# Attention, gated product and routed experts in one kernel: a unit's scores ahead of older transposes, masks on VectorE, another plan for conversions

## The chip, the cores and the metric

One core of one Trainium2 chip. The metric is device time in microseconds (us), the median of three runs. Engines are named as in the profile: PE is TensorE's matmul stream (PEld its weight loads), DVE is VectorE, ACT is ScalarE, POOL is GpSimd, SP is SyncE, which issues transfers.

## The reference

Three stages run one after the other; each consumes what the one before produced.

```
mask = q_bucket[:, :, :, None] == k_bucket[:, :, None, :]
scores = np.where(mask, scale * (q @ k^T), -1e9)          # 2 x 8 heads, 768 x 768, depth 64
attn = exp(scores - max); attn = attn / (sum + 1e-09); out = attn @ v
...
x = (a * b) @ w_out,  a = x @ w_a,  b = x @ w_b          # 1536 tokens, 512 -> 1536 -> 512, 64-bit weights
...
logits = normalised x @ normalised expert_emb / tau; one expert of 8 for each token
out[mask] = gate * (relu(x[mask] @ w1[e]) @ w2[e])       # 512 -> 1024 -> 512
```

A bucket is the signs of six projections. A query without a key in its bucket has all scores at -1e9, and so takes the mean of all v.

## The kernel before, in words

Attention is cut into 48 units: a pair of heads (8 pairs), one of the two heads, 256 of the 768 queries; six units belong to a pair, and r is the unit's number within it. A unit u has two halves t of 128 queries. The main loop makes one step for each u, and in it works on several units at once:

- `scores(u, t)` (lines 244 and 245, tile `st`): four matmuls, two chunks of keys, each with a second matmul that adds the mask through feature rows;
- `rowmax` (L254, DVE), `expo` (L260, ACT): row maximum, exponential and row sum `su`;
- `masked` (L267, L269): from the row maximum, `mk` (1 where the query has a key in its bucket) and `mc` (1/S where it hasn't); `recip` (L276, DVE): 1/sum; `normal` (L280, L282, POOL): s = r * mk, then e = e * s + mc on 128x768, twice;
- `etrans(u, m)`, m = 0, 1, 2 (L290): four transposes of e into a PSUM tile; `ehigh` (L300, ACT) and `elow` (L304, DVE) split it into a high and a low part for the product with v, `pv` (L316);
- `epilogue` and `finish` (L331, L332 on ACT; L340, xh, L342 on POOL): the two partial products of an older unit are added and split into x's high and low parts;
- in the same loop, work for the next pair: its q and k are transposed (`pt`, L162), split (L167, L170) and turned into bucket bits (`z`, L213; `ft`, L219), and v is split (`splv`, POOL); `hook(u, k)` runs steps of other jobs at five places of a step.

The jobs on hooks are four conversions of 64-bit weights to pairs of fp32r parts for the gated product, seven steps each: rest, top, low, size, guard on DVE (L542 to L561), add (L553) on POOL, and parts (L567) on ACT and POOL. A planner in `jobs` put them over steps u = 5 to 46, the POOL steps where r is 0 or 4.

Step u issues, in PE's order: scores(u, 0), the second transposes of unit u-2, scores(u, 1), the first product of unit u-3, the third transposes of u-2, the rest of u-3's product, the next pair's `pt` or `z`, and last the first transposes of unit u-1, which read what POOL's L282 writes in the same step.

Ahead of the loop the opening loads k and q of the first pair, stacks high and low parts (L372, L373), transposes them (L381), projects them (L392) and writes feature rows (L395); 28 transposes of the identity run first (`warm`, L364). After attention the gated products run (L636, L648 to L662), then the router (L767 to L854; `pos` is the place of a token in its expert's list, `sel` and `slots` the lists), the gathers (L890), their transposes (`xgt`, L906), and the experts (`hp` L929, `op` L979, result `o` L986, scattered by L987).

Every engine works in the order in which the program issues. There is no run-time scheduler.

Of the kernel before, what the change touches and what calls it, by code (L numbers as in the profile page):

```python
# [8 lines left out]
F32 = mybir.dt.float32  # L9
# [12 lines left out]
def f32(ap):  # L22
    return ap.bitcast(F32)


class Kernel:
# [69 lines left out]
    def features0(self):  # L96
        nc = self.nc
        NF, NB, D = self.NF, self.NF // 2, self.D
        pr, pp = self.pr, self.pp
        nc.vector.tensor_copy(pp[:, 0], pr)  # L100
        nc.vector.tensor_tensor(pp[:, 1], pr, f32(pp[:, 0]), ALU.subtract)
        for t in range(2):

            d = slice(D * t, D * t + D)
            for n, sign in enumerate((1.0, -1.0) if t == 0 else (-1.0, 1.0)):
                o = slice(D + n * NB, D + (n + 1) * NB)
                nc.gpsimd.tensor_scalar(self.lz0[:, t, 0, o], f32(pp[:, 0]), sign, None, ALU.mult)
                nc.gpsimd.tensor_scalar(self.lz0[d, t, 1, o], f32(pp[d, 1]), sign, None, ALU.mult)


    def attention(self, xh, xl, pools, hook):
# [121 lines left out]
        def small(tag):  # L233
            return sb.tile([128, 2], F32, tag=tag, name=tag, bufs=4)
# [29 lines left out]

        def masked(u):
            f = small("mk")
            nc.gpsimd.tensor_scalar(f, NM[u], BIG / 2, 1.0, ALU.is_lt, ALU.mult)  # L267
            c = small("mc")
            nc.gpsimd.tensor_scalar(c, NM[u], BIG / 2, 1.0 / S, ALU.is_ge, ALU.mult)  # L269
            MK[u] = (f, c)  # L270

        R = {}

        def recip(u):
            R[u] = small("r")
            nc.vector.reciprocal(R[u], SU.pop(u))  # L276

        def normal(u):
            r, (f, c) = small("s2"), MK.pop(u)
            nc.gpsimd.tensor_tensor(r, R.pop(u), f, ALU.mult)  # L280
            for t in range(2):
                nc.gpsimd.tensor_scalar(E[u, t], E[u, t], r[:, t:t + 1], c[:, t:t + 1], ALU.mult, ALU.add)  # L282

        def etrans(u, m):
            pt = ps_t.tile([128, 512], F32, tag="t", name="et")
            for cc in range(2):
                for t in range(2):
                    e = E[u, t].rearrange("p a b -> p (a b)")
                    c = 2 * m + cc
                    nc.tensor.transpose(  # L290
                        pt[:, (2 * cc + t) * 128:(2 * cc + t + 1) * 128],
                        e[:, c * 128:(c + 1) * 128], self.ident,
                    )
            eh = sb.tile([128, 512], F32R, tag="eh", name="eh", bufs=5)
            el = sb.tile([128, 512], F32R, tag="el", name="el", bufs=5)
            ET[u, m] = (eh, el, pt)
# [56 lines left out]
                return f(i + 1, *args)  # L353
            return None

        load(0, "k")
        load(0, "q", nc.scalar)
        for d in (0, 64):
            nc.gpsimd.dma_start(out=self.pr[d:d + 64], in_=self.proj)
        hook(-1, 0)  # L360

        warm = ps_t.tile([128, 512], F32, tag="t", name="warm")
        for m in range(28):
            nc.tensor.transpose(warm[:, m % 4 * 128:m % 4 * 128 + 128], self.ident, self.ident)  # L364

        P[0, 0] = sb.tile([128, 4, S], F32R, tag="p", name="p", bufs=2)
        p = P[0, 0]
        stacks = []
        for nm, h, scale in (("k", 1, 1.0), ("q", 0, float(D) ** -0.5)):
            s = sb.tile([128, NC, 2, D], F32R, tag="splv", name="stack", bufs=3)  # L370
            r = raw[0, nm][:, :, 0, :]
            nc.scalar.mul(s[:, :, h, :], r, scale)  # L372
            nc.vector.scalar_tensor_tensor(s[:, :, 1 - h, :], r, scale, f32(s[:, :, h, :]), ALU.mult, ALU.subtract)  # L373
            stacks.append(s)
        self.features0()
        for t, s in zip((1, 0), stacks):
            for half in range(2):
                pt = ps_t.tile([128, 512], F32, tag="t", name="pt0")
                for m in range(3):
                    c = 3 * half + m  # L380
                    nc.tensor.transpose(  # L381
                        pt[:, m * 128:(m + 1) * 128], f32(s[:, c]).rearrange("p a d -> p (a d)"), self.ident
                    )
                cols = slice(384 * half, 384 * half + 384)
                nc.scalar.copy(p[:, t, cols], pt[:, :384])
                nc.vector.tensor_copy(p[0:D, 2 + t, cols], pt[D * t:D * t + D, :384])
        for t in (1, 0):
            z = ps_s.tile([128, 2, 512], F32, tag="s", name="z0")
            for half in range(2):
                cols = slice(384 * half, 384 * half + 384)  # L390
                for m in range(2):
                    nc.tensor.matmul(  # L392
                        z[:D + NF, half, :384], self.lz0[:, t, m], p[:, t, cols], start=(m == 0), stop=(m == 1)
                    )
            nc.vector.tensor_scalar(  # L395
                p[D:D + NF, 2 + t].rearrange("p (a b) -> p a b", a=2), z[D:D + NF, :, :384],
                self.thr0[D:D + NF, t:t + 1], 1.0 if t == 0 else -BIG, ALU.is_gt, ALU.mult,
            )
        self.features()
        load(1, "qk")  # L400

        opening = [[(nm, half) for half in range(2)] for nm in "qk"]
        for u in range(NU + 4):
# [2 lines left out]
            act, last, tr, out = u < NU, 0 <= u - 1 < NU, 0 <= w < NU, 0 <= x < NU  # L406
            if act:
                scores(u, 0)
            if y >= 0:
                epilogue(y)  # L410
            prep = chunk(u) if 0 < u < NU else None
# [24 lines left out]
            if act:  # L436
                rowmax(u, 1)
                masked(u)
            if u == 0:
                for args in opening[1]:  # L440
                    for g in prep_t(0, *args):
                        g()
                stack_parts(0, 1, "k")
                load(0, "v")
                load(1, "v")
                hook(-1, 1)
# [32 lines left out]
                load(i + 2)  # L479
            elif r >= 4 and i + 1 < len(pairs):  # L480
                stack(i + 1, r - 4)
            if last:
                etrans(u - 1, 0)
            if act:
                expo(u, 1)
            if tr:
# [19 lines left out]
class Experts:  # L506
# [16 lines left out]
    def split64(self, src, shape, dest, scratch=None):  # L523
# [30 lines left out]


        def size():
            nc.vector.tensor_scalar(T["lo"], T["hi"], 0x7FFFFFFF, None, ALU.bitwise_and)

        def guard():
            v = f32(T["v"])  # L560
# [407 lines left out]
    def expert_out(self, e, b, n):  # L968
# [14 lines left out]
        if n < 3:  # L983
            return
        o = self.ex.tile([128, self.DM], F32, tag="o", name="o", bufs=2)
        nc.scalar.mul(o, p, self.sg[b][:, e:e + 1])  # L986
        nc.gpsimd.indirect_dma_start(  # L987
            out=self.K.out, out_offset=bass.IndirectOffsetOnAxis(ap=self.so[b][:, e:e + 1], axis=0),
            in_=o, in_offset=None, bounds_check=self.B * self.S - 1, oob_is_err=False,
# [108 lines left out]
def tile_kernel(ctx, tc, q, k, v, proj, w_a, w_b, w_out, emb, tau, w1, w2, out, dbg=None):  # L1098
# [5 lines left out]
    with tc.manual_schedule():  # L1104
# [15 lines left out]
        with tc.tile_pool(name="conv", bufs=1, side="left") as X.conv, \  # L1120
# [8 lines left out]
            def late():  # L1129
# [4 lines left out]


            plan = {(-1, 0): [jobs[0][0], jobs[1][0]], (NU - 5, 1): [j[0] for j in outs]}
            streams = [
                {"steps": [(step, m) for _, steps in jobs[n::2] for m, step in enumerate(steps)], "ready": 4,
                 "fetch": jobs[2 + n][0]} for n in range(2)
            ]  # L1140
            for u in range(4, NU):
                r = u % 6
                if r == 2:
                    continue
                for stream in streams:
                    steps = stream["steps"]
                    if steps and u >= stream["ready"] and (steps[0][1] in (3, 6)) == (r in (0, 4)):
                        step, m = steps.pop(0)
                        plan[u, 3 if m in (3, 6) else 4] = [step]
                        if m == 6 and steps:  # L1150
                            at = next(x for x in range(u + 2, u + 9) if x % 6 in (0, 1))
                            plan[at, 0] = [stream["fetch"]]
                            stream["ready"] = at + 3
                        break
                streams.reverse()
            assert not any(stream["steps"] for stream in streams)
            r, o = [j[1] for j in outs]

            def both(*steps):
                return lambda: [step() for step in steps]  # L1160

            tail = [
                r[0], r[1], both(*r[2:4]), o[0], o[1], both(*r[4:6]), both(*o[2:4]), r[6], both(*o[4:6]), o[6],
            ]
            first = [(t, f, w, h) for t in range(2) for f in range(2) for w in range(2) for h in range(2)]


# [37 lines left out]
        def after(name, fn, *args):  # L1205
            side.setdefault(name, []).append(lambda: fn(*args))
# [92 lines left out]
        def begin():  # L1299
# [4 lines left out]
        chain(("o", L, 0, 2), [(T, 0), (T, 1), [(R, 0), (T, 2)], (R, 1), (R, 2)], 2)  # L1304
        chain(("o", L, 1, 2), [
            (T, 3), (T, 4), [(R, 3), (T, 5), (X.route_norm, 0)], (R, 4), [(R, 5), (X.route_choose, 0)],
            None, None, (X.route_places, 0), None, None, [(X.route_slots, 0), (X.gather, 0, 0)],
            (X.route_gates, 0), None, None, None, None, None, (X.route_gate_slots, 0),
        ])
        chain(("o", L, 2, 1), [(T, 6), (T, 7), [(R, 6), (T, 8)], (R, 7), (R, 8)])  # L1310
# [6 lines left out]
        after(("t", 0, 0, 0), X.route_places, 1)  # L1317
        chain(("e", 0, 0, 0), [[(X.route_slots, 1), (X.gather, 0, 1)]])
        after(("h", 0, 1, 0), X.route_gates, 1)
        after(("e", 0, 0, 2), X.transpose_in, 0, 1)  # L1320
        after(("e", 0, 0, 3), X.gather, 1, 1)
        after(("e", 0, 1, 0), X.route_gate_slots, 1)
        after(("e", 0, 1, 0), X.transpose_in, 1, 0)
        after(("e", 0, 1, 1), X.transpose_in, 1, 1)
# [47 lines left out]
```

## Time and profile before

| | |
|---|---|
| median of 3 runs | 781.36 us (780.84 to 782.38) |
| the profiled execution | 781.89 us; its span 780.1 us, so 1.8 us lie outside the span |
| mean granted TensorE clock | 0.999 |
| PE busy | 756.1 us, 97% of the span |
| DVE, ACT, POOL busy | 63%, 53%, 62% |
| opening, attention | 0 to about 27 us, about 27 to 265 us |
| gated products, router, experts | to about 520, 610 and 773 us |

PE's busy time is modelled: the duration of a matmul reaches beyond the start of the next. What PE needs for a stretch is therefore read from the distance of starts in stretches without a wait, and not from the busy share. In the rows a time in brackets is the idle time of an engine just before an instruction and what ended it.

### The profile page before, as it was taken

The page shows a single profiled execution, that of the slowest core. Times are in us where ns is not written, and L with a number is a line of the kernel's source. Part 1 is how long each engine was busy: PE and PEld are TensorE (multiplying, and loading weights), DVE is VectorE, ACT ScalarE, POOL GpSimd, SP SyncE. Part 2 cuts the span into 40 slices and gives each one's busy share as a digit, 9 for nine tenths or more (in the row PEclk, how much of TensorE's full clock was granted, in tenths as well). Part 3 has the DMA queues.
Part 4 walks back from the last instruction along what each step waited for, and adds up shares of the span by engine and source line. Part 5 has one row for each costly group of instructions (what it writes and reads, how often), then busy time and mean ns, then how long its engine had stood idle before and what let it go on. Part 6 is the DMA issues. An engine that isn't in the chain of part 4 may idle for free.

```text
span 780.1 us, 13215 instructions
## 1 busy us (share of the span) xinstructions
PE 756.1 (97%) x4778; PEld 698.7 (90%) x4778; DVE 494.9 (63%) x793; ACT 414.4 (53%) x795; POOL 486.1 (62%) x532
## 2 busy tenths in 40 slices
PE   7999999999999999999999999999999999999996
PEld 6789988999889899999999999999998898899995
DVE  6789888898888754364654655533653755556551
ACT  4798898898888733321212222124343755564651
POOL 3788889889898957265463563644341865565651
PEclk9999999999999999999999999999999999999999
DMA  7875555854540303022111130053252666676620
GB/s 173 189 152 104 126 122 104 183 131 97 105 107 34 109 4 122 38 75 89 55 55 55 54 108 25 31 216 108 94 160 82 199 204 240 209 250 203 211 76 22
DMA packets 65347, 92.06 MB, mean 118 GB/s; under 512 B 28683, under 2 KB 32779, under 8 KB 65280
## 3 DMA queue, kind: packets, MB, share of 16 engines
q1 hardware_dynamic: 61088, 83.45, 38.8%
q0 software_dynamic: 2624, 7.35, 2.5%
q8 instruction: 39, 0.64, 0.3%
q10 hardware_dynamic: 1568, 0.39, 0.3%
q14 instruction: 28, 0.23, 0.1%
HBM read 66.08 MB, written 7.34 MB: 94 GB/s over the span
## 4 chain that ended last, share of the span: by engine, by line
PE 77%; POOL 11%; issue 5%; DVE 3%; ACT 1%; DMA 1%; POOLq 0%; SPq 0%; DVEq 0%; ACTq 0%
PE ab L636 24%; PE yp L662 12%; PE op L979 9%; PE hp L929 9%; POOL e L282 6%; PE et L290 6%; PE pv L316 4%; PE st L245 3%; PE st L244 3%; PE z L213 2%; PE hr L947 1%; PE lgp L745 1%; POOL xp L340 1%; PE xgt L906 1%; PE warm L364 1%
## 5 line engine op out<-in xcount | busy, mean ns | idle before, releaser
L636 PE MATMUL ab<-xh,w 128*128 128x384 f32 x768 | 204.1, 338 | 0.0
L636 PEld LDWEIGHTS ab<-xh,w 128*128 128x128 f32 x768 | 139.5, 188 | 0.8
L636 PE MATMUL ab<-xl,w 128*128 128x384 f32 x384 | 129.1, 336 | 0.0
L650 POOL TENSOR_TENSOR g<-a,g 128x384 fp32r<-128x384 f32 x48 | 52.6, 1096 | 105.2 <-ACT g L649 98.9
L885 POOL TENSOR_TENSOR w<-raw,w 128x1024 fp32r<-128x1024 f32 x36 | 87.5, 2432 | 35.2 <-ACT w L884 34.1
L254 DVE TENSOR_REDUCE nm<-st 128x1 f32<-128x768 f32 x96 | 91.3, 951 | 27.4 <-PE st L245 27.0
L290 PE MATMUL et<-ident,e 128*128 128x128 f32 x576 | 94.1, 277 | 9.9 <-POOL e L282 8.1
L662 PE MATMUL yp<-w,g 128*128 128x512 f32 x432 | 103.2, 391 | 0.3 <-POOL g L650 0.3
L304 DVE TENSOR_TENSOR el<-et,eh 128x512 fp32r<-128x512 f32 x144 | 95.3, 678 | 9.2 <-ACT eh L300 9.1
L282 POOL TENSOR_SCALAR e<-e,s,mc 128x768 f32<-128x768 f32 x96 | 94.5, 992 | 5.2
L300 ACT CAST eh<-et 128x512 fp32r<-128x512 f32 x144 | 84.5, 589 | 23.0 <-PE et L290 18.9
L662 PEld LDWEIGHTS yp<-w,g 128*128 128x128 f32 x432 | 80.4, 188 | 15.6 <-POOL g L650 0.8
L260 ACT ACTIVATE e<-st,nm 128x768 f32<-128x768 f32 x96 | 87.0, 906 | 5.0 <-DVE nm L254 2.0
L290 PEld LDWEIGHTS et<-ident,e 128*128 128x128 f32 x576 | 66.0, 140 | 22.6 <-POOL e L282 16.5
L649 ACT CAST g<-a 128x384 fp32r<-128x384 f32 x48 | 24.8, 516 | 110.4 <-DVE a L648 110.4
L979 PE MATMUL op<-w,hth 128*128 128x512 f32 x256 | 81.7, 400 | 0.0
L929 PE MATMUL hp<-xgh,w 128*128 128x256 f32 x448 | 80.7, 281 | 0.0
L316 PE MATMUL pv<-eh,splv 128*128 128x256 f32 x288 | 76.8, 296 | 0.0
L644 ACT COPY a<-ab 128x384 f32<-128x384 f32 x48 | 22.9, 478 | 97.2 <-PE ab L636 96.7
L244 PE MATMUL st<-p 128*128 128x384 f32 x192 | 73.0, 380 | 1.1 <-DVE p L395 0.7
L885 DVE TENSOR_TENSOR w<-raw,w 128x1024 fp32r<-128x1024 f32 x28 | 63.0, 2251 | 16.1 <-ACT w L884 16.1
L636 PEld LDWEIGHTS ab<-xl,w 128*128 128x128 f32 x384 | 72.3, 188 | 0.8
(192 smaller groups left out, 1549.9 us busy)
## 6 DMA issues: line engine op xcount, KB each, us to landing
raw<-in_moe_w_dram SPq DMA_DIRECT2D x32, 1024.0 KB
p<-hlq SPq DMA_DIRECT2D x15, 384.0 KB
p<-hlk SPq DMA_DIRECT2D x15, 384.0 KB
raw<-in_moe_w_a_dram SPq DMA_DIRECT2D x5, 1024.0 KB
raw<-in_moe_w_b_dram SPq DMA_DIRECT2D x5, 1024.0 KB
raw<-in_moe_w_out_dram SPq DMA_DIRECT2D x5, 1024.0 KB
raw<-in_k_dram SPq DMA_DIRECT2D x16, 192.0 KB
raw<-in_v_dram SPq DMA_DIRECT2D x16, 192.0 KB
```

Of the source, the lines that this page charges most:

```text
L244: nc.tensor.matmul(st[:, n, :384], p[:, 0, ql], p[:, 1, kl], start=True, stop=False)
L254: nc.vector.tensor_reduce(NM[u][:, t:t + 1], ST[u, t][:, :, :384], axis=AX.XY, op=ALU.max, negate=True)
L260: nc.scalar.activation(e, ST.pop((u, t))[:, :, :384], AF.Exp, bias=NM[u][:, t:t + 1], accum_out=SU[u][:, t:t + 1])
L282: nc.gpsimd.tensor_scalar(E[u, t], E[u, t], r[:, t:t + 1], c[:, t:t + 1], ALU.mult, ALU.add)
L290: nc.tensor.transpose(pt[:, (2 * cc + t) * 128:(2 * cc + t + 1) * 128], e[:, c * 128:(c + 1) * 128], self.ident,)
L304: nc.vector.tensor_tensor(el, pt, f32(eh), ALU.subtract)
L316: nc.tensor.matmul(p, w, parts[x][:, cc * 256:(cc + 1) * 256], start=(c == 0 and x == 0), stop=(c == NC - 1 and x == 1),)
L636: nc.tensor.matmul(p[:, :384], w[:, k, fs], x[:, k, cols], start=(k == 0 and n == 0), stop=(k == self.KD - 1 and n == 2),)
L662: nc.tensor.matmul(p, g[:, f, rows], w[:, f], start=(n == 0), stop=(n == 5))
L885: eng.tensor_tensor(l, raw, f32(h), ALU.subtract)
L929: nc.tensor.matmul(p[:, :256], w[:, k, fs], x[:, k], start=(n == 0), stop=(n == 3 * self.KD - 1))
L979: nc.tensor.matmul(p, h[:, 2 * n + f, rows], w[:, f], start=(n == 0 and f == 0 and m == 0), stop=(n == 3 and f == 1 and m == 2),)
```

## The change

- `etrans(w, 0)`, w = u-2, is issued just after `scores(u, 0)`. Before, the same transposes stood at the end of the step before, ahead of `scores(u, 0)`. Within `etrans` the half t is now the outer loop.
- `mk`, `mc` and the product s = r * mk are computed on DVE (L267, L269, L278 in the new numbering) and no longer on POOL.
- The planner of conversion steps is replaced by a table of steps u. POOL's steps stand at r = 0 only. For the jobs with a scratch buffer the step `size` is an Abs on ACT.
- Opening: k and q are loaded by head on two queues, with the projection between the halves (it was on POOL's queue); 22 warm transposes; queries of half 0 alone are stacked, turned and featured ahead of the first scores, and half 1 follows inside step 0.
- Router: places of tokens one slot later in the list that follows the last gated products; one transpose and one gather change places.
- The last result tile is scaled half on ACT and half on DVE.

```diff
         def masked(u):
-            nc.gpsimd.tensor_scalar(f, NM[u], BIG / 2, 1.0, ALU.is_lt, ALU.mult)
+            nc.vector.tensor_scalar(f, NM[u], BIG / 2, 1.0, ALU.is_lt, ALU.mult)
             c = small("mc")
-            nc.gpsimd.tensor_scalar(c, NM[u], BIG / 2, 1.0 / S, ALU.is_ge, ALU.mult)
+            nc.vector.tensor_scalar(c, NM[u], BIG / 2, 1.0 / S, ALU.is_ge, ALU.mult)
...
         def recip(u):
-            R[u] = small("r")
-            nc.vector.reciprocal(R[u], SU.pop(u))
+            r, (f, c) = small("r"), MK.pop(u)
+            nc.vector.reciprocal(r, SU.pop(u))
+            s = small("s2")
+            nc.vector.tensor_tensor(s, r, f, ALU.mult)
+            R[u] = (s, c)
...
-        for m in range(28):
+        for m in range(22):
...
+        stacked(1, slice(0, NC))
+        stacked(0, slice(0, 3))
+        self.features0()
+        for t, half in ((1, 0), (1, 1), (0, 0)):
+            turned(t, half)
+        featured(1, 0, 1)
+        featured(0, 0)
...
             if act:
                 scores(u, 0)
+            if tr:
+                etrans(w, 0)
...
             if u == 0:
+                stacked(0, slice(3, NC))
+                turned(0, 1)
+                featured(0, 1)
...
-            if last:
-                etrans(u - 1, 0)
...
         def size():
-            nc.vector.tensor_scalar(T["lo"], T["hi"], 0x7FFFFFFF, None, ALU.bitwise_and)
+            if scratch:
+                nc.scalar.activation(f32(T["lo"]), f32(T["hi"]), AF.Abs)
...
+            places = (
+                (3, 4, 5, 6, 6, 9, 12), (7, 10, 11, 12, 12, 13, 18), (17, 19, 21, 24, 24, 25, 36), (23, 27, 29, 30, 30, 31, 42),
+            )
...
-            None, None, (X.route_places, 0), None, None, [(X.route_slots, 0), (X.gather, 0, 0)],
+            None, None, None, (X.route_places, 0), None, [(X.route_slots, 0), (X.gather, 0, 0)],
...
-        after(("e", 0, 0, 2), X.transpose_in, 0, 1)
-        after(("e", 0, 0, 3), X.gather, 1, 1)
+        after(("e", 0, 0, 3), X.transpose_in, 0, 1)
+        after(("e", 0, 0, 2), X.gather, 1, 1)
```

On PE, from the last products of one step of the middle of attention to the second transposes of the next, before:

```order
261 L316 MATMUL pv<-el,splv 128x256
262 L290 MATMUL et<-ident,e 128x128 x4
263 L244 MATMUL st<-p 128x384
264 L245 MATMUL st<-p 128x384
265 L244 MATMUL st<-p 128x384
266 L245 MATMUL st<-p 128x384
267 L162 MATMUL pt<-ident,raw 128x128 x3
268 L290 MATMUL et<-ident,e 128x128 x4
```

And in the changed kernel:

```order
263 L318 MATMUL pv<-el,splv 128x256
264 L244 MATMUL st<-p 128x384
265 L245 MATMUL st<-p 128x384
266 L244 MATMUL st<-p 128x384
267 L245 MATMUL st<-p 128x384
268 L292 MATMUL et<-ident,e 128x128 x4
269 L162 MATMUL pt<-ident,raw 128x128 x3
270 L292 MATMUL et<-ident,e 128x128 x4
```

The four `st` matmuls of the next unit no longer stand behind the first four transposes of the unit before it.

On DVE one step from the reciprocal to the next row maximum, before (`spare` is a conversion step, not in every step):

```order
82 L276 RECIPROCAL r<-su 128x2
83 L304 TENSOR_TENSOR el<-et,eh 128x512 x2
84 L254 TENSOR_REDUCE nm<-st 128x1
85 L170 SCALAR_TENSOR_TENSOR hlk<-pt,hlk 128x384
86 L304 TENSOR_TENSOR el<-et,eh 128x512
87 L254 TENSOR_REDUCE nm<-st 128x1
```

And in the changed kernel:

```order
110 L276 RECIPROCAL r<-su 128x2
111 L278 TENSOR_TENSOR s_901<-r,mk 128x2
112 L306 TENSOR_TENSOR el<-et,eh 128x512 x2
113 L254 TENSOR_REDUCE nm<-st 128x1
114 L267 TENSOR_SCALAR mk<-nm 128x2
115 L269 TENSOR_SCALAR mc<-nm 128x2
116 L170 SCALAR_TENSOR_TENSOR hlk<-pt,hlk 128x384
117 L306 TENSOR_TENSOR el<-et,eh 128x512
118 L254 TENSOR_REDUCE nm<-st 128x1
```

Three small operations have come in, one ahead of the two `el` and two behind the second row maximum.

On POOL one step with `finish`, before:

```order
71 L267 TENSOR_SCALAR mk<-nm 128x2
72 L269 TENSOR_SCALAR mc<-nm 128x2
73 L340 TENSOR_TENSOR xp<-xp,co 128x256
74 L144 TENSOR_SCALAR xh_116<-xp 128x256
75 L342 TENSOR_TENSOR xl_118<-xp,xh_116 128x256
76 L280 TENSOR_TENSOR s_1075<-r,mk 128x2
77 L282 TENSOR_SCALAR e<-e,s_1075,mc 128x768 x2
```

And in the changed kernel:

```order
57 L342 TENSOR_TENSOR xp<-xp,co 128x256
58 L144 TENSOR_SCALAR xh_116<-xp 128x256
59 L344 TENSOR_TENSOR xl_118<-xp,xh_116 128x256
60 L284 TENSOR_SCALAR e<-e,s_1420,mc 128x768 x2
```

The three small operations have left, and nothing else of the step.

## Rows read from the trace of the kernel before

**Rows 1.** PE's waits: waiting line, what it waited for, us, times, longest

```profile
PE et L290 <- POOL e L282: 8.1, 17, 0.6
...
PE pos L789 <- DVE ohb L779: 1.2, 1, 1.2
```

**Rows 2.** Groups of instructions between 40 and 230 us

```profile
L290 PE MATMUL et<-ident,e 128*128 128x128 f32 x444 | 73.1, 278 | 6.9 <-POOL e L282 6.4
...
L282 POOL TENSOR_SCALAR e<-e,s,mc 128x768 f32<-128x768 f32 x74 | 72.3, 985 | 4.0
...
L267 POOL TENSOR_SCALAR mk<-nm 128x2 f32<-128x2 f32 x37 | 9.3, 250 | 3.7 <-DVE nm L254 1.1
...
L280 POOL TENSOR_TENSOR s<-r,mk 128x2 f32<-128x2 f32 x37 | 7.2, 194 | 10.6 <-DVE r L276 10.6
```

**Rows 3.** Timeline of POOL in one step with `finish`: start, us

```profile
142.96 1.95 POOL L282 TENSOR_SCALAR e<-e,s,mc 128x768 f32<-128x768 f32 x2
...
145.61 0.73 POOL L340 TENSOR_TENSOR xp<-xp,co 128x256 f32<-128x256 f32 x1
...
147.92 0.99 POOL L282 TENSOR_SCALAR e<-e,s,mc 128x768 f32<-128x768 f32 x1
```

**Rows 4.** Timeline of PE in the same step

```profile
144.67 0.85 PE L290 MATMUL et<-ident,e 128*128 128x128 f32 x4
...
146.06 0.49 PE L162 MATMUL pt<-ident,raw 128*128 128x128 f32 x3
146.40 0.60 PE L290 MATMUL et<-ident,e 128*128 128x128 f32 x4
```

**Rows 5.** Timeline of DVE in the same step

```profile
142.35 0.15 DVE L276 RECIPROCAL r<-su 128x2 f32<-128x2 f32 x1
142.43 1.27 DVE L304 TENSOR_TENSOR el<-et,eh 128x512 fp32r<-128x512 f32 x2
143.61 0.95 DVE L254 TENSOR_REDUCE nm<-st 128x1 f32<-128x768 f32 x1
144.47 0.55 DVE L170 SCALAR_TENSOR_TENSOR hlk<-pt,hlk 128x384 fp32r<-128x384 f32 x1
144.94 0.68 DVE L304 TENSOR_TENSOR el<-et,eh 128x512 fp32r<-128x512 f32 x1
146.33 0.96 DVE L254 TENSOR_REDUCE nm<-st 128x1 f32<-128x768 f32 x1 [0.72 <-PE st L245]
147.21 0.15 DVE L276 RECIPROCAL r<-su 128x2 f32<-128x2 f32 x1
```

**Rows 6.** Timeline of DVE: the reciprocals six units apart

```profile
137.52 0.15 DVE L276 RECIPROCAL r<-su 128x2 f32<-128x2 f32 x1
...
167.34 0.15 DVE L276 RECIPROCAL r<-su 128x2 f32<-128x2 f32 x1
```

**Rows 7.** Timeline of PE in a step with `z`

```profile
156.21 0.68 PE L213 MATMUL z<-hlq,lz 128*48 128x384 f32 x3
...
157.26 0.60 PE L290 MATMUL et<-ident,e 128*128 128x128 f32 x4
```

**Rows 8.** Summary of line 276: count, shortest, median, longest in ns, first and last start

```profile
L276 DVE RECIPROCAL r<-su x48: 144/154/157, 19.1 to 263.0; 128x2 f32<-128x2 f32 x48
```

**Rows 9.** Timelines of DVE and of POOL around 302 us

```profile
302.13 2.77 DVE L557 TENSOR_SCALAR raw<-raw 128x1024 int32<-128x1024 int32 x1
...
301.51 2.84 POOL L567 TENSOR_TENSOR w<-v,w 128x1024 fp32r<-128x1024 f32 x1
```

**Rows 10.** Timeline of DVE in the opening

```profile
8.16 2.26 DVE L386 CAST p<-pt 64x384 fp32r<-64x384 f32 x4 [0.81 <-ACT p L385]
10.46 1.94 DVE L395 TENSOR_SCALAR p<-z,thr 12x768 fp32r<-12x768 f32 x2
```

**Rows 11.** Timeline of ACT at the end

```profile
773.89 0.69 ACT L986 ACTIVATE o<-op,sg 128x512 f32<-128x512 f32 x1 [4.91 <-PEq L1002]
```

More of the change, by code (lines that the diff above doesn't have):

```diff
@@ L101, in features0 @@
         nc.vector.tensor_tensor(pp[:, 1], pr, f32(pp[:, 0]), ALU.subtract)
-        for t in range(2):
+        for t in (1, 0):
             d = slice(D * t, D * t + D)
@@ L274, in recip @@
         def recip(u):
-            R[u] = small("r")
-            nc.vector.reciprocal(R[u], SU.pop(u))
+            r, (f, c) = small("r"), MK.pop(u)
[3 more added lines that the diff above has]
+            R[u] = (s, c)
         def normal(u):
-            r, (f, c) = small("s2"), MK.pop(u)
-            nc.gpsimd.tensor_tensor(r, R.pop(u), f, ALU.mult)
+            r, c = R.pop(u)
             for t in range(2):
@@ L285, in etrans @@
             pt = ps_t.tile([128, 512], F32, tag="t", name="et")
-            for cc in range(2):
-                for t in range(2):
+            for t in range(2):
+                for cc in range(2):
                     e = E[u, t].rearrange("p a b -> p (a b)")
@@ L354, in chunk @@
             return None
[L356 to L359, printed above, removed]
+        raw[0, "k"], raw[0, "q"] = (sb.tile([128, NC, 2, D], F32, tag="raw", name="raw", bufs=4) for _ in range(2))
+        for j in range(2):
+            for nm, src, queue in (("k", self.k, nc.sync), ("q", self.q, nc.scalar)):
+                queue.dma_start(
+                    out=raw[0, nm][:, :, j, :], in_=src[0, j].rearrange("(p c) d -> p c d", c=NC)
+                )
+                if j == 0:
+                    d = 0 if nm == "k" else 64
+                    queue.dma_start(out=self.pr[d:d + 64], in_=self.proj)
         hook(-1, 0)
         warm = ps_t.tile([128, 512], F32, tag="t", name="warm")
-        for m in range(28):
+        for m in range(22):
             nc.tensor.transpose(warm[:, m % 4 * 128:m % 4 * 128 + 128], self.ident, self.ident)
@@ L367, in attention @@
         p = P[0, 0]
[L368 to L390, printed above, removed]
+        stacks = [sb.tile([128, NC, 2, D], F32R, tag="splv", name="stack", bufs=3) for _ in range(2)]
+        def stacked(t, cs):
+            s, r = stacks[t], raw[0, "qk"[t]][:, cs, 0, :]
+            scale = 1.0 if t else float(D) ** -0.5
+            nc.scalar.mul(s[:, cs, t, :], r, scale)
+            nc.vector.scalar_tensor_tensor(s[:, cs, 1 - t, :], r, scale, f32(s[:, cs, t, :]), ALU.mult, ALU.subtract)
@@ new lines, in turned, with featured @@
+        def turned(t, half):
+            pt = ps_t.tile([128, 512], F32, tag="t", name="pt0")
+            for m in range(3):
+                s = f32(stacks[t][:, 3 * half + m]).rearrange("p a d -> p (a d)")
+                nc.tensor.transpose(pt[:, m * 128:(m + 1) * 128], s, self.ident)
+            cols = slice(384 * half, 384 * half + 384)
+            nc.scalar.copy(p[:, t, cols], pt[:, :384])
+            nc.vector.tensor_copy(p[0:D, 2 + t, cols], pt[D * t:D * t + D, :384])
+        def featured(t, *halves):
+            if len(halves) == 2:
+                z = ps_s.tile([128, 2, 512], F32, tag="s", name="z0")
+            else:
+                z = ps_t.tile([128, 512], F32, tag="t", name="z0").rearrange("p (a c) -> p a c", a=1)
+            for n, half in enumerate(halves):
@@ L391, in attention @@
                 for m in range(2):
                     nc.tensor.matmul(
-                        z[:D + NF, half, :384], self.lz0[:, t, m], p[:, t, cols], start=(m == 0), stop=(m == 1)
+                        z[:D + NF, n, :384], self.lz0[:, t, m], p[:, t, 384 * half:384 * half + 384],
+                        start=(m == 0), stop=(m == 1),
                     )
+            cols = slice(384 * halves[0], 384 * halves[-1] + 384)
             nc.vector.tensor_scalar(
-                p[D:D + NF, 2 + t].rearrange("p (a b) -> p a b", a=2), z[D:D + NF, :, :384],
+                p[D:D + NF, 2 + t, cols].rearrange("p (a b) -> p a b", b=384), z[D:D + NF, :, :384],
@@ L556, in size @@
         def size():
-            nc.vector.tensor_scalar(T["lo"], T["hi"], 0x7FFFFFFF, None, ALU.bitwise_and)
+            if scratch:
+                nc.scalar.activation(f32(T["lo"]), f32(T["hi"]), AF.Abs)
+            else:
+                nc.vector.tensor_scalar(T["lo"], T["hi"], 0x7FFFFFFF, None, ALU.bitwise_and)
         def guard():
@@ L985, in expert_out @@
         o = self.ex.tile([128, self.DM], F32, tag="o", name="o", bufs=2)
-        nc.scalar.mul(o, p, self.sg[b][:, e:e + 1])
+        if e == self.E - 1 and b == self.B - 1:
+            nc.scalar.mul(o[:, :256], p[:, :256], self.sg[b][:, e:e + 1])
+            nc.vector.tensor_scalar(o[:, 256:], p[:, 256:], self.sg[b][:, e:e + 1], None, ALU.mult)
+        else:
+            nc.scalar.mul(o, p, self.sg[b][:, e:e + 1])
         nc.gpsimd.indirect_dma_start(
@@ L1136, in tile_kernel @@
             plan = {(-1, 0): [jobs[0][0], jobs[1][0]], (NU - 5, 1): [j[0] for j in outs]}
[L1137 to L1156, printed above, removed]
+            places = (
+                (3, 4, 5, 6, 6, 9, 12), (7, 10, 11, 12, 12, 13, 18), (17, 19, 21, 24, 24, 25, 36), (23, 27, 29, 30, 30, 31, 42),
+            )
+            for (_, steps), us in zip(jobs, places):
+                for m, u in enumerate(us):
+                    plan.setdefault((u, 3 if m in (3, 4, 6) else 4), []).append(steps[m])
+            plan[13, 0], plan[19, 0] = [jobs[2][0]], [jobs[3][0]]
             r, o = [j[1] for j in outs]
@@ L1160, in both @@
                 return lambda: [step() for step in steps]
-            tail = [
-                r[0], r[1], both(*r[2:4]), o[0], o[1], both(*r[4:6]), both(*o[2:4]), r[6], both(*o[4:6]), o[6],
-            ]
+            tail = [r[0], r[1], both(*r[2:5]), o[0], o[1], r[5], both(*o[2:5]), r[6], o[5], o[6]]
             first = [(t, f, w, h) for t in range(2) for f in range(2) for w in range(2) for h in range(2)]
```

## The prediction

> **What bounds the kernel now.** I read the engines' shares first, then PE's waits, then the attention stage by groups, and last one step of it by timelines. PE is busy for 97% of the span, so what can be had is what PE waits for, and the waits name one place: in 17 cases it waits for POOL's `e`, 8.1 us together [rows 1]. Between 40 and 230 us this is nearly all the idle time ahead of the transposes, 6.4 of 6.9 us [rows 2]. The idle time understates the loss, because a matmul's modelled duration runs on into the gap: the four `et` behind `e` take 0.85 us, the four that wait for nothing 0.60 [rows 4].
>
> So attention is a loop over several engines, and the timelines of one step show it. On POOL one `e` pair starts at 142.96, the next at 147.92, and POOL's work between them has hardly a gap [rows 3]. The pair ends at 144.91 (142.96 + 1.95); the transposes `et` issued at 144.67 end just behind it, and only then come the next unit's scores, whose row maximum starts on DVE at 146.33, after DVE had been idle for 0.72 us; the reciprocal follows at 147.21, and with it `s` and the next pair [rows 3 to 5]. The distance of reciprocals is the period: 147.21 - 142.35 = 4.86 us [rows 5]. Six units of a stretch without much conversion on POOL take 167.34 - 137.52 = 29.82 us [rows 6]. Four of these steps hold three `pt` transposes and two hold six `z` matmuls; four at 4.86 leave 29.82 - 19.44 = 10.38 for the two, 5.19 each.
>
> What does PE itself need? The six `z` take 157.26 - 156.21 = 1.05 [rows 7], the three `pt` 146.40 - 146.06 = 0.34 [rows 4]. If the `z` steps are PE's own pace, a `pt` step needs 5.19 - 0.71 = 4.48 on PE. A `pt` step therefore has at most 4.86 - 4.48 = 0.38 us to give, a `z` step nothing.
>
> **The transposes behind the scores.** No work is added. The scores no longer wait for `e`; the row maximum, the reciprocal and `s` come earlier by what the wait was, and `e` has until the scores are through (four `st` and their successors) to be ready. The cycle e, transposes, scores, row maximum, e of [rows 3 to 5] is cut: it now spans two steps. What takes over is the sum of one engine's work.
>
> **Masks and s on DVE.** POOL loses 0.25 for `mk`, a like amount for `mc` and 0.19 for `s` in each unit [rows 2], about 0.7 with gaps; its 4.96 per step with `finish` falls to near 4.3, so POOL is no longer the fullest. DVE's step is added up from starts: reciprocal to `el` 0.08, two `el` 1.18, row maximum 0.86, low part 0.47, `el` 0.60 (its 0.68 less the overlap that the pair shows), row maximum and the step to the reciprocal 0.88: 4.07 us [rows 5]. Three operations of 128x2 come to it. The trace has one DVE operation of that shape, the reciprocal, 0.15 long and followed after 0.07 to 0.08 by the next [rows 5]. `mk` and `mc` depend on the row maximum and `s` on the reciprocal, so a part of the full 0.15 shows each time; three times 0.15 is 0.45, three times 0.08 is 0.24. I take 0.45: DVE 4.52. It is then the fullest engine, just above PE's 4.48. For handing over between engines I add 0.1, since `el` waits for ACT's `eh` in places: 4.62 in a `pt` step. The `z` step stays at 5.19.
>
> Six units: 4 x 4.62 + 2 x 5.19 = 28.86, so 0.96 less than 29.82. The steps in which all stages overlap, from the fifth unit until the last pairs have nothing more to prepare, are some 38 of 48, 6.3 times six: **-6.1 us**. Bounds: 0 (another loop holds 4.86) and 0.38 x 4 x 6.3 = -9.6 (PE's own pace).
>
> **Conversion steps.** The same steps run, in other units. POOL's go where r = 0, which has neither `finish` nor `splv`; six of DVE's go to ACT. On a DVE that is full each remaining step shows whole, on the POOL of before it was POOL's that showed. I take these as even, 0, with bounds of 2 us to either side; the cover is DVE's and POOL's slack in `z` steps, about 0.5 us each.
>
> **Opening.** Ahead of the first scores DVE makes four casts in 2.26 and two threshold passes over 768 columns in 1.94 us [rows 10]. One cast (0.57) and half of a pass (0.48) move behind the scores: **-1.0**. They come back in step 0, with some stacking for DVE and ACT and three transposes and two matmuls for PE; if nothing covers them there, the gain is 0. Six warm transposes fewer cost nothing as long as the loads are what the first real ones wait for.
>
> **Router, end.** PE waits 1.2 us at `pos` [rows 1]; matmuls of the last gated products now stand ahead of it. At most 1.2; the lists of tokens come later by as much, and the exchanged transpose and gather may cost some tenths: I take **-0.7**, bounds 0 and -1.2. The last scaling takes 0.69 on ACT [rows 11]; in halves on two engines about 0.35 to 0.4: **-0.3**.
>
> **Sum.** -6.1 - 1.0 - 0.7 - 0.3 = -8.1 against the profiled execution's 781.89 (span 780.1 and 1.8 outside): 773.8. That execution lies 0.5 above the median of 781.36, so for the median 773.3.
>
> **A price that the sum leaves out.** At 302.13 a DVE tensor_scalar on SBUF lasts 2.77 us; it ends at 304.90, a little over half a microsecond after POOL's operation, which ran from 301.51 to 304.35 [rows 9]. It stood still for POOL. `mk` and `mc` are tensor_scalars on SBUF too, `s` reads two SBUF tiles. And they come when POOL is busy: from the reciprocal, the second row maximum ends after 2.2 us (143.61 + 0.95 against 142.35) and with `s` ahead of it 2.35, while `e`, started at about 0.3, ends at 2.25 (1.95 long) and `xp` follows it [rows 3, 5]; so `mk` would meet an `xp` that has just begun. On the other side, the 48 reciprocals of 128x2 took 144 to 157 ns each, none longer, and POOL, almost without a gap in such steps, worked beside many of them [rows 3, 8]. The wait of such a small operation lies between 0 and the 0.73 of a whole `xp` [rows 3]; I take 0, by the row of the same shape, and keep the other end as a rival.
>
> [...]
>
> **Rivals.**
> *Masks stand still for POOL.* Where r = 0 POOL has neither `finish` nor `splv`, so three of the four `pt` steps of six units are open to it. A whole `xp` each time makes DVE's `pt` step 4.52 + 0.73 = 5.25, 0.63 above 4.62, and the two `z` steps 5.36 (DVE's `ft` is taken as 0.1 longer than the low part), 0.17 above 5.19: 2.2 in six units, 14 in 6.3 times six, and the time is 787: slower. Half of it (0.37) adds 1.1 in six units, 7 in all: 780, no gain. It decides from 0.43 us a step on, which gives back the 8.1. For it: [rows 9], the meeting of `mk` with `xp`, and a DVE without slack. Against it: [rows 8], and that DVE could come first and hold up POOL, which has slack. Chances: under half of an `xp` (775 to 779) 0.10, half to 0.45 us (780 to 783) 0.08, more 0.20.
> *The steps don't shrink.* ACT or the chain exponential, copies, `eh`, `el`, row maximum holds the `pt` step at 4.86: only opening, router and end are left, -2.0, 779.4. For it: DVE already waits for ACT's `eh` and the sum of 4.52 leaves no room for any wait. Against: DVE's 0.72 of idle time in a step waits for the scores and not for ACT [rows 5]. Chance 0.08, half of it above 779.8.
>
> **Numbers.** The forecast, 770 to 776, has 0.54. Faster by over 0.2% (under 779.8; 0.2% is about what three runs tell from no change): 0.54 + 0.10 + 0.04 = 0.68; within 0.2%: 0.04 + 0.08 = 0.12; slower: 0.20. The range of 8 in 10 reaches from 769, where PE's own pace is nearly met, to 785, which takes in the mild half of the first rival and leaves out its worst; the forecast's own range is 770 to 776.
>
> **What the profile after would show.** Right: PE's wait for `e` at the transposes all but gone; reciprocals of `pt` steps 4.6 apart, six units in about 28.9; POOL with a gap ahead of each `e` pair; DVE with hardly an idle time in `pt` steps; the opening's threshold passes done near 11.4 in place of 12.4; `pos` without the 1.2. Wrong: `mk`, `mc` or `s` with durations well over 0.15 and their starts tied to ends of POOL's operations; DVE's groups unchanged but its steps at 4.9 or more; or `eh` as what DVE waits for.

## The result, and the profile after

The changed kernel takes 792.45 us (median of 4 runs, 791.66 to 792.91) against 781.23 before: ratio 1.0142, 95% interval 1.0126 to 1.0157. It is slower by 11 us where 773.3 was forecast; the range ended at 785, and the time lies beyond the 787 of the rival that ended on this side. The profiled execution has a span of 789.8 us.

The page of the changed kernel: its busy line.

```profile
PE 761.1 (96%) x4772; PEld 699.2 (89%) x4772; DVE 531.8 (67%) x934; ACT 415.8 (53%) x802; POOL 445.5 (56%) x386
```

POOL has lost 41 us of work and DVE has gained 37, though the three operations that went over are short. Where DVE's time went is in the groups of instructions between 40 and 230 us of the changed kernel, which answer to [rows 2]:

```profile
L284 POOL TENSOR_SCALAR e<-e,s,mc 128x768 f32<-128x768 f32 x70 | 68.2, 984 | 59.0 <-DVE s L278 35.3 <-PE et L292 12.0 <-ACT eh L302 6.4
L254 DVE TENSOR_REDUCE nm<-st 128x1 f32<-128x768 f32 x70 | 66.1, 945 | 0.0
...
L267 DVE TENSOR_SCALAR mk<-nm 128x2 f32<-128x2 f32 x35 | 23.2, 662 | 1.2
...
L269 DVE TENSOR_SCALAR mc<-nm 128x2 f32<-128x2 f32 x34 | 6.5, 190 | 0.0
...
L278 DVE TENSOR_TENSOR s<-r,mk 128x2 f32<-128x2 f32 x35 | 5.6, 160 | 1.2
```

`mk` takes 662 ns on average, for 256 numbers. `mc`, the same operation just behind it, takes 190. DVE has no idle time left ahead of its row maxima (0.0). POOL, which was busy for 162.7 of these 190 us before, nearly as long as DVE (164.8), is busy for 125.8 now and idles 59.0 us ahead of `e`, mostly for `s` from DVE; DVE is busy for 186.1.

Why `mk` is long can be read off two timelines. DVE of the changed kernel (start, us), the `mk` of three units:

```profile
143.80 0.17 DVE L267 TENSOR_SCALAR mk<-nm 128x2 f32<-128x2 f32 x1
...
149.19 1.30 DVE L267 TENSOR_SCALAR mk<-nm 128x2 f32<-128x2 f32 x1
...
154.84 0.76 DVE L267 TENSOR_SCALAR mk<-nm 128x2 f32<-128x2 f32 x1
```

POOL of the changed kernel beside them:

```profile
144.06 0.52 POOL L144 TENSOR_SCALAR splv<-raw 128x384 fp32r<-128x384 f32 x1 [0.21 <-PE pv L318]
...
147.27 1.95 POOL L284 TENSOR_SCALAR e<-e,s,mc 128x768 f32<-128x768 f32 x2 [1.59 <-ACT eh L302]
149.18 1.29 POOL L574 TENSOR_TENSOR spare<-spare,r 128x512 int32<-128x512 int32 x1
152.93 1.95 POOL L284 TENSOR_SCALAR e<-e,s,mc 128x768 f32<-128x768 f32 x2 [2.46 <-DVE s L278]
154.85 0.72 POOL L342 TENSOR_TENSOR xp<-xp,co 128x256 f32<-128x256 f32 x1
```

Both long `mk` begin with an operation of POOL and end just behind it (150.49 and 150.47, 155.60 and 155.57); the short one fell into a gap of POOL, but for its first 0.06 us. Both long ones began 0.03 to 0.04 us before the end of POOL's `e` (149.22 and 154.88), and it was still POOL's next operation that ran first, whole; the trace has 20 such units of 48. The summary of the line shows the spread over all 48 units: shortest 168 ns, median 571, longest 1303.

```profile
L267 DVE TENSOR_SCALAR mk<-nm x48: 168/571/1303, 14.0 to 272.3; 128x2 f32<-128x2 f32 x48
```

By stages, from the reciprocals (L276): the first stands at 21.64 us in place of 19.13, so the opening lost 2.5. The 38 units from the fifth to the 43rd reciprocal take 204.81 us (42.07 to 246.88) in place of 195.15 (39.89 to 235.04): 9.7 lost. At the 43rd it is 11.8 behind; the span is longer by 9.7 in all, so the rest of the kernel gives 2.1 back.

PE's waits in the changed kernel, beside [rows 1]:

```profile
PE et L292 <- DVE el L306: 6.9, 13, 0.7
PE pt L162 <- DVE hlq L170: 4.5, 6, 1.7
PE pt L387 <- DVE stack L381: 2.6, 2, 2.2
...
PE hr L971 <- ACT xgh L933: 0.8, 1, 0.8
...
PE pos L813 <- DVE ohb L803: 0.2, 1, 0.2
```

The 8.1 us of waiting for POOL's `e` are gone, as the moved transposes were to bring; in their place PE waits for DVE (`el`, `hlq`).

### The profile page after: what moved, and what is told of

It is laid out like the page before. It is cut to its first block, busy times and chain, and to the rows that moved or that the text cites. A ratio compares the mean times of both kernels' runs of the same rounds, so it can differ in the third digit from the quotient of the medians.

```text
span 789.8 us, 12981 instructions
## 1 busy us (share of the span) xinstructions
PE 761.1 (96%) x4772; PEld 699.2 (89%) x4772; DVE 531.8 (67%) x934; ACT 415.8 (53%) x802; POOL 445.5 (56%) x386
## 5 line engine op out<-in xcount | busy, mean ns | idle before, releaser
L292 PE MATMUL et<-ident,e 128*128 128x128 f32 x576 | 89.6, 278 | 7.9 <-DVE el L306 6.9
L318 PE MATMUL pv<-el,splv 128*128 128x256 f32 x288 | 73.0, 283 | 0.0
```

Of the source, the lines that this page charges most:

```text
L292: nc.tensor.transpose(pt[:, (2 * cc + t) * 128:(2 * cc + t + 1) * 128], e[:, c * 128:(c + 1) * 128], self.ident,)
L318: nc.tensor.matmul(p, w, parts[x][:, cc * 256:(cc + 1) * 256], start=(c == 0 and x == 0), stop=(c == NC - 1 and x == 1),)
```

## The experiments

Two explanations were set against each other. *Standstill*: an operation of DVE that meets a running operation of POOL is blocked to its end. *Other parts*: the moved transposes or the new places of the conversion steps slow attention, and `mk` is only long because it waits on an engine that has time; or DVE simply has too many operations, whatever POOL does. All kernels below compute the whole reference. For each the table gives the time, its ratio to the runs of before beside it, the first reciprocal, and the 38 units between the fifth and the 43rd reciprocal. The runs of before beside them had medians of 781.56 (e1 to e4), 781.91 (e5 to e8) and 781.30 (e9, e10), so some tenths between these groups say nothing.

| kernel | us | ratio (95%) | first reciprocal | 38 units |
|---|---|---|---|---|
| before | 781.23 | | 19.13 | 195.15 |
| changed | 792.45 | 1.0142 (1.0126 to 1.0157) | 21.64 | 204.81 |
| e1 masks and s on POOL | 772.05 | 0.9873 (0.9852 to 0.9894) | 21.30 | 186.00 |
| e2 before, masks and s on DVE | 793.42 | 1.0150 (1.0129 to 1.0170) | 19.00 | 205.96 |
| e3 masks at the reciprocal | 776.76 | 0.9938 (0.9918 to 0.9958) | 21.46 | 189.16 |
| e4 masks by one column | 779.89 | 0.9976 (0.9963 to 0.9988) | 21.47 | 192.05 |
| e5 as e1, opening of before | 771.81 | 0.9864 (0.9839 to 0.9890) | 18.95 | 185.96 |
| e6 before, transposes moved | 773.45 | 0.9891 (0.9863 to 0.9919) | 18.75 | 186.52 |
| e7 as e1, stack early | 769.29 | 0.9832 (0.9806 to 0.9858) | 18.63 | 186.10 |
| e8 as e1, 28 warm | 773.16 | 0.9879 (0.9854 to 0.9905) | 22.28 | 186.12 |
| e9 as e7, last scaling whole | 768.99 | 0.9833 (0.9809 to 0.9856) | 18.74 | 185.97 |
| e10 as e7, s on DVE | 772.45 | 0.9877 (0.9855 to 0.9900) | 18.53 | 188.53 |

**e1: everything but the masks and s.**

```diff
-            nc.vector.tensor_scalar(f, NM[u], BIG / 2, 1.0, ALU.is_lt, ALU.mult)
+            nc.gpsimd.tensor_scalar(f, NM[u], BIG / 2, 1.0, ALU.is_lt, ALU.mult)
...
-            nc.vector.tensor_tensor(s, r, f, ALU.mult)
+            nc.gpsimd.tensor_tensor(r, R.pop(u), f, ALU.mult)
```

> The changed kernel with mk, mc and s back on POOL, the rest as changed. Theory L (mk on DVE stands still for POOL's running operation): mk took 0.66 us on average in place of 0.17, about 24 us of DVE time over 48 units; without it attention falls back under the time of before, about 776 to 781 us in all, with the opening still some 2.5 us late. Theory M (it is the moved transposes or the conversion table that slows attention, the long mk only fills a DVE that would wait anyway): no better than 788.

Measured: 772.05, 20.4 us less than the changed kernel and better than the standstill theory had it. The rest of the change is a gain of 1.3%, and these three small operations turn it into a loss. The other-parts theory (788 or more) falls.

**e2: the masks and s alone**, moved to DVE in the kernel before, with the two functions of the diff above.

> The kernel before with only mk, mc and s on DVE. Theory L: mk of 0.5 us or more, DVE nearly without idle time, slower than before by 5 to 12 us. Theory M: the masks alone change little, 779 to 783 us.

Measured: 793.42, 11.9 us slower than the runs of before beside it (781.56), at the upper end. Groups of instructions of e2 between 40 and 230 us:

```profile
L254 DVE TENSOR_REDUCE nm<-st 128x1 f32<-128x768 f32 x70 | 66.1, 945 | 0.5
...
L267 DVE TENSOR_SCALAR mk<-nm 128x2 f32<-128x2 f32 x35 | 22.0, 630 | 1.2
```

The same long `mk` with the order and the conversion plan of before, so neither is its cause.

**e3: the same operations, one row maximum later**, where POOL mostly waits for `s`.

```diff
                 rowmax(u, 1)
-                masked(u)
...
             if last:
+                masked(u - 1)
                 recip(u - 1)
```

> The changed kernel with mk and mc issued on DVE one row maximum later, just ahead of the reciprocal, where POOL waits for s and so holds nothing. The same instructions, the same count. Theory L: mk 0.17 to 0.25 us, the time 776 to 782. Theory F (DVE has too much work, whatever POOL does): the same number of DVE operations, so 790 or more.

Measured: 776.76, 15.7 us less than the changed kernel with the same instructions on the same engine. Group of e3 between 40 and 230 us:

```profile
L267 DVE TENSOR_SCALAR mk<-nm 128x2 f32<-128x2 f32 x38 | 7.1, 187 | 0.0
```

`mk` takes 187 ns in place of 662. Over 38 units that is 38 x 0.475 = 18 us less of DVE's time, and the 38 units are 15.65 us shorter: on an engine with hardly any idle time most of the standstill had been on the path. Not all of it is gone: six of these 38 `mk` still meet an operation of POOL (0.28 to 0.74 us). The theory of too many operations (790 or more) falls for these 15.7 us. It may hold for what is left: against e1, with the same three operations on POOL, e3 is slower by 4.7.

**e4: the same place, other shape.**

```diff
+            for t in range(2):
+                n = NM[u][:, t:t + 1]
+                nc.vector.tensor_scalar(f[:, t:t + 1], n, BIG / 2, 1.0, ALU.is_lt, ALU.mult)
+                nc.vector.tensor_scalar(c[:, t:t + 1], n, BIG / 2, 1.0 / S, ALU.is_ge, ALU.mult)
```

> The changed kernel with mk and mc written one column at a time: four operations of 128x1 at the same place in place of two of 128x2. [...] If every tensor_scalar on SBUF stands still for POOL: mk still 0.6 us on average, 792 or more. Theory F: 795 or more.

Measured: 779.89, 12.6 less than the changed kernel with two more DVE operations in each unit. Groups of e4 between 40 and 230 us:

```profile
L269 DVE TENSOR_SCALAR mk<-nm 128x1 f32<-128x1 f32 x74 | 10.0, 146 | 0.0
L270 DVE TENSOR_SCALAR mc<-nm 128x1 f32<-128x1 f32 x74 | 10.0, 143 | 0.0
```

No 128x1 operation in e4's timelines waits (120 of them take 0.14 or 0.15 us), though POOL runs beside them. Timelines of e4, one `mk` of DVE and POOL's `xp`:

```profile
146.07 0.14 DVE L269 TENSOR_SCALAR mk<-nm 128x1 f32<-128x1 f32 x1
...
146.04 0.74 POOL L343 TENSOR_TENSOR xp<-xp,co 128x256 f32<-128x256 f32 x1
```

So the standstill belongs to the form of the operation on DVE: two columns stand still for `xp`, one column does not. Two columns alone do not bring it: the 48 reciprocals of 128x2 of the changed kernel took 143 to 166 ns. Between 40 and 230 us `mk` takes 0.66 us on average with two columns in the changed kernel and 0.15 with one in e4. What it is in the form that makes the one stand still and not the other, no run here shows.

**e5, e7, e8: the opening.** e5 is e1 with the whole opening of before. e7 is e1 with one line moved:

```diff
         featured(0, 0)
+        stacked(0, slice(3, NC))
         self.features()
...
             if u == 0:
-                stacked(0, slice(3, NC))
                 turned(0, 1)
```

e8 is e1 with `range(28)` warm transposes in place of 22.

> The changed kernel with mk, mc and s on POOL and with the whole opening of before. The first reciprocal stood at 19.1 us before and at 21.3 with the masks back on POOL, so if the opening is the loss: about 2.2 us less than 772.05, near 769.9. If what comes late in the opening is made up later in attention: 771.5 to 772.5.

> The changed kernel with mk, mc and s on POOL, and the second half of the queries stacked ahead of the loop in place of behind the second row maximum of step 0. If PE's 2.0 us wait for that stack and the low clock behind it are the opening's loss: the wait falls under 0.5, the transposes at 16.4 us run at 0.11 us each, and the time is 767.5 to 769.5. If the opening is late for another reason (loads, the first features): 771.5 or more.

> The changed kernel with mk, mc and s on POOL, and 28 warm transposes as before in place of 22. If the low clock behind 16 us comes from the fewer warm transposes: full clock there, 770 to 771. If it comes from PE's wait in step 0: the same low clock, 772 to 773.

Measured: e5 771.81, the same as e1 within the runs' scatter, so the first of its two expectations failed and the second held: the reciprocal comes 2.35 us earlier, but only 1.2 are left at the fifth. e7 769.29, 2.8 less than e1. e8 773.16, by its ratio the same as e1. PE's timeline of e1 in step 0:

```profile
14.90 0.52 PE L385 MATMUL pt<-ident,stack 128*128 128x128 f32 x3 [1.97 <-DVE stack L379]
15.99 0.58 PE L397 MATMUL z<-p,lz 128*76 128x384 f32 x2 [0.57 <-ACT p L387]
16.41 2.56 PE L162 MATMUL pt<-ident,raw 128*128 128x128 f32 x12
...
19.23 0.53 PE L245 MATMUL st<-p 76*128 76x384 f32 x1
19.55 0.53 PE L244 MATMUL st<-p 128*128 128x384 f32 x1
```

And of e7:

```profile
12.36 0.49 PE L385 MATMUL pt<-ident,stack 128*128 128x128 f32 x3
13.41 0.57 PE L397 MATMUL z<-p,lz 128*76 128x384 f32 x2 [0.57 <-ACT p L387]
...
16.75 0.34 PE L245 MATMUL st<-p 76*128 76x384 f32 x1
16.93 0.34 PE L244 MATMUL st<-p 128*128 128x384 f32 x1
```

In e1 PE stands 1.97 us before three transposes of the second half of the queries, because DVE stacks that half only behind the second row maximum (14.41 to 14.76), and PE has everything else of step 0 queued behind them. Behind that wait it is slower for a while: the `st` matmuls above start 0.32 us apart in e1, in e7 0.18. In the changed kernel, where PE waits 2.23 us for the same stack, to 14.68, the granted clock is 1.00 from 14 to 15 us, 0.51, 0.50 and 0.50 in the next three microseconds, 0.78 in the one after and 1.00 from 19 to 20. The windows from 10 to 27 us give the mean granted clock, 0.90 in e1 and 1.00 in e7:

```profile
10.00:27.00 17.00, 13.60 (x76) 10.87 (x76) 13.05 (x24) 9.30 (x22) 6.09 (x15) 0.90 0.69 150
```

```profile
10.00:27.00 17.00, 14.85 (x88) 11.56 (x89) 14.90 (x26) 11.42 (x25) 8.36 (x19) 1.00 0.76 171
```

(after the length of the window: busy us of PE, PEld, DVE, ACT and POOL, then the clock, the DMA share and GB/s.) e8, with six warm transposes more, has the same wait (1.97) and the same 0.90: the number of warm transposes is not the reason. By what the clock falls behind such a wait, no run shows.

**e6: the moved transposes alone**, on the kernel before.

```diff
                 scores(u, 0)
+            if tr:
+                etrans(w, 0)
...
-            if last:
-                etrans(u - 1, 0)
```

> The kernel before with only the first transposes moved behind the next unit's scores (and the half t outer in them). If this move is what shortens the steps: 38 units in 187 to 190 us in place of 195, the time 773 to 777. If the conversion table does it: 193 us or more, 779 to 782.

Measured: 773.45, and 186.52 us for the 38 units in place of 195.15. The move alone brings 8.6 us there. With the conversion table besides (e1) it is 186.00: the table adds 0.5 in these units. Behind them e1 is 2.2 shorter than e6 (543.7 from the 43rd reciprocal to the end, against 545.9), by the table, the router and the end together.

**e9, e10: two small parts on e7.** In e9 the last tile is scaled on ACT alone; in e10 only s moves to DVE.

> The kernel of e7 (masks and s on POOL, second half of the queries stacked early) with the last result tile scaled by ACT alone, as before. In the traces the scatter's issue comes 0.97 us after the start of the last scaling before and 1.27 after the change. If DVE's half runs behind ACT's and not beside it: 0.97 again, and 0.2 to 0.4 us less than 769.3. If the halves help: 0.3 more.

> The kernel of e7 with s = r * mk alone on DVE, mk and mc staying on POOL. s comes just behind the reciprocal, where POOL waits for it. If only an operation that meets a running POOL operation stands still: s 0.16 us, POOL loses 0.2 to 0.3 per unit, and the time is 768 to 769.5. If DVE, with hardly any room, pays for any further operation: 48 x 0.1 to 0.18 us, 771 to 774.

e9: 768.99 against 769.29, a difference within the scatter of the runs; the trace shows its sign. End of e7, with halves:

```profile
760.90 0.47 ACT L1010 ACTIVATE o<-op,sg 128x256 f32<-128x256 f32 x1 [4.91 <-PEq L1029]
761.41 0.48 DVE L1011 TENSOR_SCALAR o<-op,sg 128x256 f32<-128x256 f32 x1 [10.91 <-ACT o L1010]
762.17 0.97 POOL L1014 DMA_INDIRECT out_dram<-o,so  x1 [4.91 <-DVE o L1011]
```

End of e9, in one piece:

```profile
760.96 0.69 ACT L1008 ACTIVATE o<-op,sg 128x512 f32<-128x512 f32 x1 [4.91 <-PEq L1024]
761.92 0.98 POOL L1009 DMA_INDIRECT out_dram<-o,so  x1 [4.60 <-ACT o L1008]
```

DVE's half starts when ACT's has ended, and the row names ACT's `o` as what released it: the program puts a wait on ACT ahead of it. The halves share two tiles, `o`, which both write, and `op`, which both read; which of the two the wait is for, no run shows. So the scatter is issued 1.27 us behind the first scaling and not 0.96.

e10: 772.45, 3.2 slower than e7, in the range of its second expectation, but the trace does not bear out the reason, and the premise of the first failed: POOL does not always wait where `s` comes. Group of e10 between 40 and 230 us, and the summary of its line:

```profile
L278 DVE TENSOR_TENSOR s<-r,mk 128x2 f32<-128x2 f32 x38 | 9.3, 244 | 4.1 <-POOL mk L267 0.3
```

```profile
L278 DVE TENSOR_TENSOR s<-r,mk x48: 160/161/748, 18.8 to 253.9; 128x2 f32<-128x2 f32 x48
```

14 of the 48 `s` take 0.20 us or more, and each of these ends 0.01 to 0.02 us behind an operation of POOL. The longest, on DVE and on POOL:

```profile
68.20 0.15 DVE L276 RECIPROCAL r<-su 128x2 f32<-128x2 f32 x1
68.45 0.75 DVE L278 TENSOR_TENSOR s<-r,mk 128x2 f32<-128x2 f32 x1
```

```profile
68.17 1.01 POOL L151 TENSOR_TENSOR splv<-raw,splv 128x384 fp32r<-128x384 f32 x1
```

So `s`, with both inputs in SBUF, stands still too (to 69.20, POOL's operation to 69.18), and the reciprocal ahead of it, beside the same operation of POOL, does not. In the 38 units the standstills of `s` add up to 3.4 us of DVE's time, and these units are 2.4 us longer than those of e7 (188.53 against 186.10). So e10 does not show what a further operation costs without a standstill.

## Why the prediction was wrong

**What failed first is one choice.** The wait of `mk` for POOL was taken as 0, "by the row of the same shape", the reciprocals [rows 8]. The measured wait is 0.662 - 0.17 = 0.49 us on average, with whole operations of POOL (0.76 for an `xp` of 0.72). The right row was the one of the same operation, the tensor_scalar of 2.77 us [rows 9], and not the one of the same shape. The trace of before had more such rows inside attention: one conversion step on DVE, four times in the kernel with the same shape, took from 0.42 to 1.01 us.

```profile
L550 DVE TENSOR_SCALAR r<-spare x4: 416/642/1008, 83.1 to 227.2; 128x512 int32<-128x512 uint32 x4
```

e3 and e4 show that this wait was most of the loss: nearly without it the changed kernel is at 776.76. Of all the kernels e3 comes nearest to what was forecast, and it agrees with the terms of the forecast but for the opening: its 38 units are 6.0 us shorter than before (forecast 6.1), what follows them 1.1 shorter (forecast 1.0), and its fifth reciprocal stands 1.7 later (41.61 against 39.89) where the opening was to bring 1.0. That e1 with 772.05 lies 1.2 us from the forecast is luck: it has the masks on POOL, its units gain 9.2 in place of 6.1, and its opening loses.

**The rival named it and was too cheap.** 787 was worked out with r = 0 taken as free. But r = 0 is where the table puts POOL's conversion steps, and in the seven such units `mk` takes 0.82 to 1.30 us. In the 38 units the rival comes to 14 - 6.1 = 7.9 us more than before, and 9.7 were measured; the rest of the gap is the opening, which lost 2.5 where 1.0 was to be gained. (The rival's step of 5.25 also leaves out the 0.1 for handing over that the 4.62 and the half wait contain.)

**Masks on DVE, cost without a wait.** e3 has 189.16 / 38 = 4.98 us a unit, e1 without the masks on DVE 186.00 / 38 = 4.89. So the three operations cost 3.2 us in 38 units, of which some 1.3 may be the six `mk` that still wait. In e4, where none waits, the five operations cost 192.05 - 186.00 = 6.0. Putting them on DVE is a loss in every place that was tried.

**Transposes behind the scores.** Right in mechanism and nearly in size. The -6.1 is with the masks on DVE; without them PE's 4.48 is the fuller engine in the prediction's sums, which gives the lower bound of -9.6 and leaves 3.5 for the masks. Measured: -8.6 for the move alone (e6) and 3.2 for the masks (e3).

**Conversion table.** Taken as 0; e5 is 1.6 faster than e6, from which it differs by the table, the router and the end. By the paragraph on router and end, these make 0.9 - 0.3 = 0.6 of it, so an estimate for the table is -1.0, inside the bound of 2.

**Opening.** Forecast -1.0, with 0 as the bound if nothing covers the moved half. The second of the first four `st` matmuls did come earlier, at 10.78 in place of 12.46, but the first reciprocal 2.2 later (e1). The step that failed is the bound: the moved half is not merely uncovered. PE takes its instructions in the order of issue, so its three transposes hold up all of step 0 (1.97 us in e1), and the low clock came with the stall (0.90 on average from 10 to 27 us in e1, e8 and the changed kernel; 1.00 in e7 without the stall). e7 shows that one line's place decides: -0.5 at the first reciprocal in place of +2.2.

**Router, end.** Router right by its waits: `pos` waits 0.2 in place of 1.2, and `hr` 0.8 in place of `xgt` 0.7; -0.9 where -0.7 was taken. End wrong in sign: +0.3 for -0.3 in the rows (the times of e7 and e9 do not tell them apart), since the two halves run one behind the other.

## What to carry to other kernels

Before work goes from POOL to DVE, look at what POOL runs at that very moment and what it runs next, and price an operation of a form that stands still (here a tensor_scalar or tensor_tensor of two columns in SBUF) with the whole of POOL's operation (`mk` took 0.76 us beside an `xp` of 0.72) and not with its own length (0.17); a row of the same operation outweighs a row of the same shape. On an engine with hardly any idle time small operations come back in the total even without a standstill (6.0 / 38 = 0.16 us a unit in e4), so look first for an engine that waits anyway. When a part of the opening is put off, look at what stands behind it in the queue of the engine that needs it.

## What was not expected of the hardware

- A tensor_scalar of 128x2 on DVE stood still for a POOL operation for as long as that ran (1.30 us beside 1.29); four of 128x1 in place of two did not (0.14 to 0.15 us beside an `xp` of 0.74), nor did a reciprocal of 128x2 (0.15 beside a `splv` of 1.01). A tensor_tensor of 128x2 from two tiles in SBUF did (0.75 beside the same `splv`).
- A `mk` that began 0.03 us before the end of POOL's `e` did not run next: POOL's following operation went first, whole (1.29 us).
- In e1 a stall of 1.97 and one of 0.57 us in the opening were followed by `st` matmuls 0.32 us apart in place of 0.18, at a mean granted clock of 0.90 from 10 to 27 us; in e7, without the first stall, that clock was 1.00. In the changed kernel, behind a stall of 2.23, it was 0.50 from 16 to 18 us.
